# Attention and a two-layer MLP on one core: w_in loaded in parts between the first pairs, v of pair 0 on another queue, fewer zero matmuls, decay rows in front of q and k

## The chip, the core and the metric

The kernel runs on one core of a Trainium2 chip. Five engines run side by side, each through its own instructions in order: TensorE (PE), VectorE (DVE), ScalarE (ACT), GpSimd (POOL) and SyncE (SP). A transfer (DMA) is issued by SP, ACT or POOL into a queue of that engine, and all transfers run on 16 DMA engines. The metric is the device time of one execution in microseconds (us). The time of a kernel is the median of its runs.

## What is computed

Attention over 8 x 8 heads, 576 positions and 64 columns, with a decay from the running sum of a gate s, followed by two matrix products with a gated activation between them:

```python
cum = np.cumsum(np.maximum(s, 0.0), axis=-1)
bias = -(cum[:, :, :, None] - cum[:, :, None, :])
scores = np.where(causal, -1e9, q @ k.T / np.sqrt(D) + np.minimum(bias, 0.0))
attn = softmax(scores)
x = (attn @ v)                      # as 4608 tokens x 512
h = x @ w_in                        # 512 x 2048
out = (h * np.clip(h + 3, 0, 6) / 6) @ w_out
```

## The kernel before

**Units.** The 64 heads are worked as 32 pairs, two heads of one batch each. For a pair, q and k (f32, 288 KB each) come into one tile `qkf` (three buffers) and v (288 KB) into a slot of `v_f` (three slots, pair modulo 3). POOL casts q and k to f16 (`cast_qk`, L174), PE transposes them in two groups (`transpose_group`, L251), and DVE copies the result out of PSUM into `qkT`, again three slots. Rows 64 to 67 of a slot hold the decay: a running sum, split into three f16 parts, and its negative. They are worked out at the start for all heads. Pair 0 gets them straight from the tile `aug` (L475 to L482), pairs 1 to 9 from a scratch tensor in DRAM that `store_aug` (L486) fills in two halves and `load_aug` (L166) reads. Pairs from 10 on get theirs by another way.

`scores_bank` (L281) multiplies k and q of one head in four PSUM banks, ACT takes the exp of each bank into `Pm` (L299), and POOL clears what lies above the diagonal (L304). `attend` (L329) multiplies by v, whose cast `cast_v` is DVE's for pairs 0 to 3 and POOL's later, and divides. `x_transpose` (L365) puts the pair's result into `xT`. The first product, `m1` (L412), reads `xT` and `w_in`; the second, `m2`, reads `w_out`. Weights are cast from f32 to f16 on the way in, by DMAs that POOL issues: `w_in` in two halves of 1,024 columns (`load_w_in`, L391), each with four blocks of 128 rows, `w_out` in four parts.

**Order.** It is written out by hand (a manual schedule): each engine runs its instructions in the order in which the program names them. The start goes so:

1. SP loads s, and q and k of pairs 0 and 1; ACT loads the mask rows and the unit matrix. PE runs 18 zero matmuls (`keep_warm(18)`).
2. The decay is worked out on DVE. SP and ACT each issue four small DMAs for pair 0's rows (L475 to L482). Then SP asks for q and k of pair 2 and v of pair 0 (L483, L484).
3. POOL casts pair 0, PE transposes it, POOL stores the first half of the decay rows, SP loads them for pairs 1 and 2 and then v of pair 1, POOL casts pair 1, and PE runs `keep_warm(12)` (L659 to L670).
4. `first_tasks(p)` (L501) for pairs 0 to 3: scores of both heads, attention of the head before, the transposes of pair p + 1, and the loads ahead. Within pair 0, `casts` casts pair 2 behind pair 0's masks. Within pair 1 it casts v of pair 1, then q and k of pair 3, and then both halves of w_in are asked for (L524, L525).
5. `load_pair(6)`, casts of pair 4, three parts of w_out, four zero matmuls, the last head of pair 3 and its `x_transpose`.
6. The first eight column blocks of the first product over tokens 0 to 511 run in one piece (L685). After that attention and products are woven: `weave` (L617) takes attention tasks by their costs in proportion to the products' tasks.

`load_pair` (L492) is used for pairs 4 to 9 and names q and k first, then v, and the decay rows last, all on SP.

Of the kernel before, what the change touches and what calls it, by code (L numbers as in the profile page):

```python
# [16 lines left out]
def kernel(  # L17
# [10 lines left out]
    nc = tc.nc  # L28
# [9 lines left out]
    KC = DM // 128  # L38
# [6 lines left out]
    PTD = 10  # L45
# [7 lines left out]
    def bank():  # L53
        return psum.tile([128, 512], F32, tag="M", bufs=2, name="bank")
# [38 lines left out]
    w_in_sb = [  # L93
        cpool.tile([128, KC, 1024], F16, tag=f"c_win{h}", name=f"w_in{h}") for h in range(2)
    ]
# [11 lines left out]
        out=s8, in0=s_sb, scalar1=0.0, scalar2=8.0, op0=ALU.max, op1=ALU.mult  # L107
# [3 lines left out]
        out=c8, data0=s8, data1=s8, initial=0.0, op0=ALU.add, op1=ALU.max  # L111
# [12 lines left out]
        out=kaug[:, 2, :], in0=r1, in1=kaug[:, 1, :], op=ALU.subtract  # L124
# [18 lines left out]
    def load_qk(p, *engs):  # L143
        b, h0 = (2 * p) // H, (2 * p) % H
        t = work.tile([128, NTR, 2, D], F32, tag="qkf", bufs=3, name=f"qkf{p}")
        for i, src in enumerate((q, k)):
            rows = src[b, h0:h0 + 2].rearrange("h s d -> (h s) d")
            engs[i % len(engs)].dma_start(
                out=t[:, :, i, :], in_=rows.rearrange("(t p) d -> p t d", p=128)
            )  # L150
        qk_f[p] = t

    def load_v(p, eng):
        b, h0 = (2 * p) // H, (2 * p) % H
        sl = p % NS
        for hh in range(2):
            eng.dma_start(
                out=v_f[:, sl, hh, 0:4, :],
                in_=v[b, h0 + hh, 0:512].rearrange("(t p) d -> p t d", p=128),
            )  # L160
        eng.dma_start(
            out=v_f[0:64, sl, :, 4, :],
            in_=v[b, h0:h0 + 2, 512:SEQ].rearrange("h p d -> p h d"),
        )

    def load_aug(p, eng):  # L166
        sl = p % NS
        src, c0 = (aug_drams[0], p * W2) if 2 * p < NA else (aug_drams[1], p * W2 - NA * SEQ)
        eng.dma_start(
            out=qkT[64:68, sl, 0:2 * W2].rearrange("r (i c) -> r i c", i=2),  # L170
            in_=src[:, :, c0:c0 + W2].rearrange("i r c -> r i c"),
        )

    def cast_qk(p):  # L174
        t = work.tile([128, NTR, 2, D], F16, tag="qkh", bufs=2)
        nc.gpsimd.tensor_copy(out=t, in_=qk_f.pop(p))  # L176
        qk_h[p] = t
# [57 lines left out]
    def cast_v(p):  # L235
        sl = p % NS
        copy = nc.vector.tensor_copy if p < 4 else nc.gpsimd.tensor_copy
        copy(out=v_h[:, sl, :, :, 0:D], in_=v_f[:, sl])  # L238
# [12 lines left out]
    def transpose_group(p, g):  # L251
        t0, t1 = ((0, 5), (5, 9))[g]
        n = (t1 - t0) * 128
        pT = half_bank(p < 4)
        src = qk_h[p]
        for t in range(t0, t1):
            c = (t - t0) * 128
            transpose_tile(pT[:, c:c + 128], src[:, t, :, :], t == t0, t == t1 - 1)
        sl = p % NS
        c0 = t0 * 128  # L260
        for dst, r0 in ((qT, 0), (kT, 64)):
            nc.vector.tensor_copy(out=dst[0:64, sl, c0:c0 + n], in_=pT[r0:r0 + 64, 0:n])  # L262
        if g == 1:
            qk_h.pop(p)
# [64 lines left out]
    def attend(hd):  # L329

        p, hh = hd // 2, hd % 2
        sl = p % NS
        P = Pm[:, hd % NS, :]
        if hh == 0:
            O_tiles[p] = psum.tile([128, 2, 512], F32, tag="O", bufs=1, name=f"O{p}")
        O = O_tiles[p]
        for qt in range(5):
            for kt in range(qt + 1):
                c = BLOCK[kt, qt]
                nc.tensor.matmul(  # L340
                    out=O[:, hh, qt * VW:qt * VW + D + 1],
                    lhsT=P[:, c:c + 128],
                    rhs=v_h[:, sl, hh, kt, 0:D + 1],
                    start=(qt == 0),
                    stop=(qt == 4 and kt == 4),
                )
        if hh == 1:
            Ov = O_tiles.pop(p)[:, :, 0:5 * VW].rearrange("p h (t e) -> p h t e", t=5)
            r = work.tile([128, 2, 5, 1], F32, tag="r")
            nc.vector.reciprocal(out=r, in_=Ov[:, :, :, D:D + 1])  # L350
            xs = work.tile([128, 5, 2, D], F16, tag="xs", name=f"xs{p}")
            nc.vector.tensor_tensor(  # L352
                out=xs.rearrange("p t h d -> p h t d"),
                in0=Ov[:, :, :, 0:D],
                in1=r.to_broadcast([128, 2, 5, D]),
                op=ALU.mult,
            )
            x_tiles[p] = xs
# [6 lines left out]
    def x_transpose(p):  # L365
        b, hp = p // (H // 2), p % (H // 2)
        xs = x_tiles.pop(p)
        if by_dma(p):

            nc.sync.dma_start(  # L370
                out=xT[:, hp, b * SEQ:b * SEQ + 640].rearrange("p (t c) -> p t c", c=128),
                in_=xs.rearrange("p t h d -> p (t h d)"),
                transpose=True,
            )
            return
        pX = half_bank(p < 3)
        for qt in range(5):
            nc.tensor.matmul(
                out=pX[:, qt * 128:(qt + 1) * 128],
                lhsT=xs[:, qt, :, :],  # L380
                rhs=ident,
                is_transpose=True,
                start=(qt == 0),
                stop=(qt == 4),
            )
        nc.vector.tensor_copy(out=xT[:, hp, b * SEQ:(b + 1) * SEQ], in_=pX[:, 0:SEQ])
# [1 line left out]

    def load_w_in(h):  # L391
        nc.gpsimd.dma_start(
            out=w_in_sb[h],
            in_=moe_w_in[:, h * 1024:(h + 1) * 1024].rearrange("(kc p) f -> p kc f", p=128),
        )

    def load_w_out(c):
# [64 lines left out]
    def keep_warm(n):  # L462
        pw = bank()
        for i in range(n):
            nc.tensor.matmul(  # L465
                out=pw, lhsT=warm[:, 0:128], rhs=warm, start=(i == 0), stop=(i == n - 1)
            )
# [11 lines left out]
    for hh in range(2):  # L479
        c0, c1 = hh * SEQ, (hh + 1) * SEQ  # L480
        nc.sync.dma_start(out=kT[65:66, 0, c0:c1], in_=kaug[hh:hh + 1, 1, :])
        nc.scalar.dma_start(out=kT[66:67, 0, c0:c1], in_=kaug[hh:hh + 1, 2, :])  # L482
    load_qk(2, nc.sync)  # L483
    load_v(0, nc.sync)  # L484

    def store_aug(i, h0, h1, eng):  # L486
        eng.dma_start(
            out=aug_drams[i].rearrange("i r (h t) -> h (i r) t", t=SEQ),
            in_=aug[h0:h1].rearrange("h i r t -> h (i r) t"),
        )  # L490

    def load_pair(p):  # L492
        load_qk(p, nc.sync)
        load_v(p, nc.sync)
        if p < PTD:
            load_aug(p, nc.sync)

    def scores(hd):
        return [(lambda bi=bi: scores_bank(hd, bi), 400) for bi in range(4)]

    def first_tasks(p):  # L501

        def loads():
            if p == 0:
                load_qk(3, nc.sync)
                load_v(2, nc.sync)
            elif p > 1:
                load_pair(p + 2)  # L510

        def v_first():
            cast_v(0)
            load_v(3, nc.sync)
            load_aug(3, nc.sync)
            store_aug(1, NA, 2 * PTD, nc.sync)

        def casts():
            if p > 0:
                cast_v(p)  # L520
            if p < 2:
                cast_qk(p + 2)
            if p == 1:
                load_w_in(0)  # L524
                load_w_in(1)  # L525

        tr = [[], []]
        if p < 3:
            tr = [[(lambda: transpose_group(p + 1, 0), 640)],
                  [(lambda: transpose_group(p + 1, 1), 512)]]  # L530
        t = scores(2 * p)
        if p == 1:
            t += [(v_first, 0), (lambda: attend(0), 1200)]
        t += tr[0]
        if p > 0:
            t += [(lambda: attend(2 * p - 1), 1200)]
        t += scores(2 * p + 1) + [(casts, 0)] + tr[1]
        if p > 0:
            t += [(lambda: x_transpose(p - 1), 640)]
            t += [(lambda: attend(2 * p), 1200)]  # L540
        return [(loads, 0)] + t
# [125 lines left out]
        load_aug(p, nc.sync)  # L667
    load_v(1, nc.sync)
    cast_qk(1)
    keep_warm(12)  # L670
    for p in range(4):
        run(first_tasks(p))
    load_pair(6)
    cast_qk(4)
    cast_v(4)
# [59 lines left out]
```

The softmax here doesn't subtract the row's maximum and nothing guards it: scores larger than these inputs give would overflow.

## Time and profile before

| | |
|---|---|
| runs | 6, from 375.24 to 377.73 us, median 376.86 us |
| profiled execution | 375.24 us, of which the span of the profile is 373.5 us |
| clock granted to TensorE | 0.997 |
| PE busy | 353.8 us, 95% of the span |
| ACT, DVE, POOL busy | 209.4, 188.4 and 149.9 us |
| moved by DMA | 59.36 MB, 159 GB/s over the span |

PE is the busiest engine, and from about 100 us on it is busy almost without a break. Idle time of another engine costs nothing unless PE waits for it. By ten-microsecond stretches PE is busy 7.65 us from 40 to 50 us, 9.00 from 50 to 60, 9.53 from 60 to 70 and 8.71 from 70 to 80, and mostly 9.8 to 10.0 afterwards. In the first 34 us it has gaps of up to 1.45 us.

A few times of the start, from the timeline: the 18 zero matmuls run from 1.39 to 7.87 us, pair 0 is cast from 7.50 to 9.26, the twelve zero matmuls start at 10.85, the first score matmul at 13.45, the first exp at 13.82, and the first product with w_in at 34.08.

Times are in us from the start of the span. In the lines of the profile PEld is PE's weight load, and a name with a q behind it (SPq, ACTq, POOLq) is the issuing side of that engine. Matmuls are pipelined and their ends are modelled.

### The profile page before, as it was taken

How to read it: one execution, taken by the hardware profiler on the slowest of the kernel's cores; microseconds unless marked ns; L12 is line 12 of the kernel's file. 1: busy time of each engine (PE TensorE's matmuls, PEld its weight loads, DVE VectorE, ACT ScalarE, POOL GpSimd, SP SyncE). 2: the span in 40 equal slices, each digit the busy share in tenths (PEclk: the TensorE clock that was granted, in tenths of full speed). 3: DMA queues.
4: the chain of work that ended last, by engine and by line, in shares of the span. 5: the costliest groups of instructions: out<-in, count | busy, mean ns of one | idle time of the engine just before them, and what ended most of it. 6: DMA issues, size and time to landing. Idle time of an engine off the chain costs nothing.

```text
span 373.5 us, 7607 instructions
## 1 busy us (share of the span) xinstructions
PE 353.8 (95%) x2784; PEld 218.7 (59%) x2784; DVE 188.4 (50%) x331; ACT 209.4 (56%) x404; POOL 149.9 (40%) x378
## 2 busy tenths in 40 slices
PE   6778879999999899999999999999999999999995
PEld 2465555556666566566656665666566656555542
DVE  4685765666632455345533553455345545554531
ACT  4465764237884677477747774677467715443310
POOL 6582444354566355445544444444444300000000
PEclk9999999999999999999999999999999999999998
DMA  9699999946999999998999889889995101010012
GB/s 162 141 176 208 205 208 209 235 124 150 185 199 210 215 218 191 210 225 189 190 232 210 176 177 236 201 180 195 219 178 110 49 29 45 13 56 30 28 57 85
DMA packets 184526, 59.36 MB, mean 159 GB/s; under 512 B 177840, under 2 KB 178064, under 8 KB 184488
## 3 DMA queue, kind: packets, MB, share of 16 engines
q1 hardware_dynamic: 182392, 54.42, 69.6%
q0 software_dynamic: 1680, 4.27, 6.4%
q8 instruction: 22, 0.36, 0.4%
q10 hardware_dynamic: 416, 0.19, 0.2%
q14 instruction: 16, 0.13, 0.1%
HBM read 37.49 MB, written 9.62 MB: 126 GB/s over the span
## 4 chain that ended last, share of the span: by engine, by line
PE 83%; ACT 5%; DVE 4%; DMA 3%; issue 2%; POOL 1%; SPq 0%; ACTq 0%; POOLq 0%
PE bank L423 26%; PE po L445 23%; PE S L291 10%; PE bank L445 9%; PE O L340 7%; PE bankS L423 4%; ACT Pm L299 3%; DMA qkT<-xb 2%; ACT trl L431 1%; DMA qkf<-in_k_dram 1%; DVE gT L432 1%; DVE qkT L262 1%; PE bank L465 1%; PE bankY L423 1%; DVE xs L352 1%
## 5 line engine op out<-in xcount | busy, mean ns | idle before, releaser
L299 ACT ACTIVATE Pm<-S 128x384 f16<-128x384 f32 (+2 forms) x256 | 115.5, 508 | 57.3 <-PE S L291 52.9
L432 DVE SCALAR_TENSOR_TENSOR gT<-trl,bank 128x512 f16<-128x512 f32 x123 | 84.5, 687 | 102.2 <-ACT trl L431 101.9
L304 POOL TENSOR_SCALAR_AFFINE_SELECT Pm<-Pm 128x128 f16<-128x128 f16 (+2 forms) x256 | 79.3, 312 | 133.5 <-ACT Pm L299 123.7
L431 ACT ACTIVATE trl<-bank,bias 128x512 f32<-128x512 f32 x123 | 85.2, 693 | 77.3 <-PE bank L423 75.5
L423 PE MATMUL bank<-xT,w_in 128*128 128x512 f16 x492 | 126.4, 382 | 0.7
L445 PE MATMUL po<-w_out_sb,gT 128*128 128x512 f16 x416 | 104.3, 379 | 0.0
L423 PEld LDWEIGHTS <-w_in 128*128 128x128 f16 x576 | 78.5, 146 | 33.4 <-issue 2.4
L445 PEld LDWEIGHTS <-gT 128*128 128x128 f16 x576 | 52.3, 98 | 48.6 <-issue 0.3
L291 PE MATMUL S<-qkT 128*128 128x320 f16 (+4 forms) x448 | 70.2, 261 | 7.1 <-ACT Pm L299 4.1
L291 PEld LDWEIGHTS <-qkT 128*128 128x128 f16 x448 | 40.9, 98 | 36.6 <-issue 4.3
L340 PEld LDWEIGHTS <-Pm 128*128 128x128 f16 x960 | 38.3, 97 | 13.2 <-POOL Pm L304 1.8
L340 PE MATMUL O<-v_h,Pm 128*128 128x65 f16 x960 | 40.8, 193 | 1.5 <-POOL Pm L304 1.3
L445 PE MATMUL bank<-w_out_sb,gT 128*128 128x512 f16 x160 | 39.4, 379 | 0.0
L352 DVE TENSOR_TENSOR xs<-O,r 128x640 f16<-128x640 f32 x32 | 26.4, 825 | 1.1
L454 DVE TENSOR_SCALAR osb<-po 128x512 f32<-128x512 f32 x26 | 17.9, 688 | 15.2 <-PE po L445 14.9
L222 POOL CAST xb<-qkf 128x1152 f16<-128x1152 f32 x22 | 25.3, 1149 | 0.0
L238 POOL CAST v_h<-v_f 128x640 f16<-128x640 f32 x28 | 20.1, 719 | 3.1 <-DMA v_f<-in_v_dram 3.1
L454 DVE TENSOR_SCALAR osb<-bank 128x512 f32<-128x512 f32 x10 | 6.9, 691 | 26.0 <-PE bank L445 26.0
L176 POOL CAST t<-qkf 128x1152 f16<-128x1152 f32 x10 | 12.4, 1241 | 12.2 <-DMA qkf<-in_k_dram 12.2
L423 PE MATMUL bankS<-xT,w_in 128*128 128x512 f16 x64 | 16.4, 379 | 0.0
L431 ACT ACTIVATE trl<-bankS,bias 128x512 f32<-128x512 f32 x16 | 11.0, 688 | 8.0 <-PE bankS L423 8.0
L432 DVE SCALAR_TENSOR_TENSOR gT<-trl,bankS 128x512 f16<-128x512 f32 x16 | 11.0, 688 | 6.8 <-ACT trl L431 6.8
(49 smaller groups left out, 120.2 us busy)
## 6 DMA issues: line engine op xcount, KB each, us to landing
qkf<-in_q_dram SPq DMA_DIRECT2D x32, 288.0 KB, 4.3
qkf<-in_k_dram SPq DMA_DIRECT2D x32, 288.0 KB, 4.2
out_dram<-osb SPq DMA_DIRECT2D x36, 256.0 KB, 2.8
v_f<-in_v_dram SPq DMA_DIRECT2D x64, 128.0 KB, 4.1
w_in<-in_moe_w_in_dram POOLq DMA_DIRECT2D x2, 1024.0 KB, 12.0
w_out_sb<-in_moe_w_out_dram POOLq DMA_DIRECT2D x4, 512.0 KB, 7.9
v_f<-in_v_dram SPq DMA_DIRECT2D x32, 32.0 KB, 2.7
qkT<-xb SPq DMA_TRANSPOSE x22, 4.9
```

The source lines that it names most:

```text
L222: nc.gpsimd.tensor_copy(out=x.rearrange("p (i t) c -> p t i c", i=2)[:, :, :, 0:D], in_=qk_f.pop(p))
L238: copy(out=v_h[:, sl, :, :, 0:D], in_=v_f[:, sl])
L291: nc.tensor.matmul(out=S[:, c:c + hi - lo], lhsT=kT[:, sl, off + 128 * kt:off + 128 * (kt + 1)], rhs=qT[:, sl, off + lo:off + hi], start=( ...
L299: nc.scalar.activation(out=P[:, p0:p0 + n], in_=S[:, 0:n], func=AF.Exp, scale=0.125, bias=0.0)
L304: nc.gpsimd.affine_select(out=view, in_=view, pattern=pattern, compare_op=ALU.is_ge, fill=0.0, base=0, channel_multiplier=-1,)
L340: nc.tensor.matmul(out=O[:, hh, qt * VW:qt * VW + D + 1], lhsT=P[:, c:c + 128], rhs=v_h[:, sl, hh, kt, 0:D + 1], start=(qt == 0), stop=(qt ...
L352: nc.vector.tensor_tensor(out=xs.rearrange("p t h d -> p h t d"), in0=Ov[:, :, :, 0:D], in1=r.to_broadcast([128, 2, 5, D]), op=ALU.mult,)
L423: nc.tensor.matmul(out=ph, lhsT=w_in_t[f // 8][:, kc, f % 8, :], rhs=xT[:, kc, n * 512:(n + 1) * 512], start=(kc == 0), stop=(kc == KC - 1),)
L431: nc.scalar.activation(out=trl, in_=ph, func=AF.Relu, bias=bias3[:, 0:1], scale=1.0)
L432: nc.vector.scalar_tensor_tensor(out=gT[n][:, f, :], in0=trl, scalar=6.0, in1=ph, op0=ALU.min, op1=ALU.mult)
L445: nc.tensor.matmul(out=po, lhsT=gT[n][:, f, t4 * 128:(t4 + 1) * 128], rhs=w_out_sb[:, f, :], start=(f == 0), stop=(f == NF - 1),)
L454: nc.vector.tensor_scalar_mul(out=osb, in0=po, scalar1=1.0 / 6.0)
```

## The change

Four edits, all in the start of the kernel and in `load_pair`:

- `load_w_in` takes a range of row blocks. The first block of the first half is asked for by POOL after the cast of pair 1, the second in `casts` of pair 0, in front of the cast of pair 2. The other two blocks and the second half are asked for where both halves stood.
- v of pair 0 goes on ACT's queue, and its three issues stand ahead of the load of pair 2.
- `keep_warm(12)` becomes `keep_warm(6)`.
- `load_pair` names the decay rows first, then q and k, then v.

```diff
-    def load_w_in(h):
+    def load_w_in(h, k0=0, k1=KC):
         nc.gpsimd.dma_start(
-            out=w_in_sb[h],
-            in_=moe_w_in[:, h * 1024:(h + 1) * 1024].rearrange("(kc p) f -> p kc f", p=128),
+            out=w_in_sb[h][:, k0:k1, :],
+            in_=moe_w_in[:, h * 1024:(h + 1) * 1024].rearrange("(kc p) f -> p kc f", p=128)[
+                :, k0:k1, :
+            ],
         )
...
+    load_v(0, nc.scalar)
     load_qk(2, nc.sync)
-    load_v(0, nc.sync)
...
     def load_pair(p):
+        if p < PTD:
+            load_aug(p, nc.sync)
         load_qk(p, nc.sync)
         load_v(p, nc.sync)
-        if p < PTD:
-            load_aug(p, nc.sync)
...
             if p > 0:
                 cast_v(p)
+            if p == 0:
+                load_w_in(0, 1, 2)
             if p < 2:
                 cast_qk(p + 2)
             if p == 1:
-                load_w_in(0)
+                load_w_in(0, 2, 4)
                 load_w_in(1)
...
     cast_qk(1)
-    keep_warm(12)
+    load_w_in(0, 0, 1)
+    keep_warm(6)
     for p in range(4):
         run(first_tasks(p))
```

## The prediction

> **What bounds the kernel now.** I read the page first: TensorE (PE) is 95% busy over a span of 373.5 us, so a change in the loads can only pay where PE waits. Of PE's waits most lie before 34 us (2.0 us on exps, 1.6 on casts, 1.2 + 0.8 on xs, 0.9 before the zero matmuls) and between 42 and 80 us, and from 90 us on the list holds 1.5 us in all. All that the change touches lies before 45 us, so the chain of waits there comes next, start, length and what:
>
> ```profile
> 10.30 0.50 DVE qkT L262
> 10.81 0.05 issue
> 10.85 2.76 PE bank L465 x12
> 13.62 0.18 PE S L291 x2
> 13.79 0.02 issue
> 13.82 3.29 ACT Pm L299 x8
> 17.11 0.32 PE S L291 x2
> 17.43 1.47 POOL t L176
> 18.89 0.05 issue
> 18.94 0.45 PE pTm L247 x5
> ```
>
> No load stands in it. After pair 0's transposes come twelve zero matmuls, eight exps of pair 0 back to back, then GpSimd's (POOL's) cast of pair 2, on which PE's next transposes wait. From there the chain alternates between PE, exps and VectorE (DVE) until 34.24, where the first product with w_in starts straight after the last transpose of x. The timeline of POOL shows why its cast is in the chain: POOL has no gap from 14.38 to 19.94 us.
>
> ```profile
> 14.38 3.08 POOL L304 TENSOR_SCALAR_AFFINE_SELECT Pm<-Pm 128x256 f16<-128x256 f16 x8 [3.26 <-ACT Pm L299]
> 17.41 1.47 POOL L176 CAST t<-qkf 128x1152 f16<-128x1152 f32 x1
> 22.32 1.14 POOL L176 CAST t<-qkf 128x1152 f16<-128x1152 f32 x1
> 23.41 1.54 POOL L392 DMA_DIRECT2D w_in<-in_moe_w_in_dram x2
> 40.59 1.14 POOL L176 CAST t<-qkf 128x1152 f16<-128x1152 f32 x1 [9.24 <-DMA qkf<-in_k_dram]
> ```
>
> The last line is the second place: the cast of pair 4 waits 9.24 us for its load and ends at 41.73, and the weight loads of pair 4's transposes wait for it:
>
> ```profile
> 41.79 0.62 PEld L247 LDWEIGHTS <-t 128*128 128x128 f16 x9 [0.16 <-POOL t L176]
> ```
>
> Only 0.16 us here, but with nothing to spare. The DMA view of 23 to 36 us says why pair 4 is late (queue, packets, MB, share of the engines; then issues with their time to landing): w_in's queue q0 holds the engines, and SyncE's (SP's) q1 gets a fifth.
>
> ```profile
> q0 software_dynamic: 899, 1.81, 79.9%
> q1 hardware_dynamic: 1549, 0.48, 20.0%
> ...
> w_in<-in_moe_w_in_dram POOLq DMA_DIRECT2D x2, 1024.0 KB, 12.0
> qkf<-in_q_dram SPq DMA_DIRECT2D x1, 288.0 KB, 15.0
> ```
>
> SP is held inside its issues meanwhile (timeline of SP):
>
> ```profile
> 24.95 2.72 SPq L148 DMA_DIRECT2D qkf<-in_k_dram  x1
> 27.76 11.26 SPq L157 DMA_DIRECT2D v_f<-in_v_dram  x2
> ```
>
> The two w_in halves land 9.0 and 15.0 us after their issues, at 32.4 and 39.2; their users start at 34.08 and 42.4, so w_in itself is not waited for.
>
> **What the Trainium skill says.** "DMA: Bandwidth & Descriptors", section "Queues, rings and completion order": each DMA engine goes round its queues packet by packet. The trace agrees: 899 large packets of q0 took 79.9% while 1,549 small ones of q1 took 20.0%. "Trainium Kernel Development and Optimization", "Key Constraints": issuing from another engine "only saves the sequencer's issue time", as the transfers share the same 16 engines. So v on ScalarE's (ACT's) queue frees SP, but brings no bandwidth. "TensorE: Matmul & The Clock Gate", Part 1: the clock falls after an idle window of about 3.4 us; in the trace weight loads of zero matmuls stand 0.43 us apart until 6 us, and PE then runs at full rate through idle stretches of up to 1.45 us.
>
> **The change part by part**, against the profiled execution (375.24 us: span 373.5 and 1.74 around it).
>
> *Half as many zero matmuls.* Twelve take 2.76 us with the drain, 0.216 us each in the chain's spacing (2.6/12), so six fewer let PE go 1.3 us sooner, at 12.15. But pair 0's scores also need the decay rows: the last row issued on ACT's queue starts at 9.54 and takes 3.3 us, so 12.85; SP's last starts at 9.79, and with 2.7 to 3.3 us lands at 12.5 to 13.1. The first score matmul stood at 13.45, its weights at 13.24. So the gain is 0.15 to 0.6 us; I take 0.35. What is late next is the rows. PE's new idle gap is under 1 us, far from the clock's window.
>
> *v of pair 0 on ACT's queue.* Three issues of 0.6 us (ACT's own in the rows: 0.54 to 0.66) from 10.20 end at about 12.1; queued behind them are pair 0's exps, which start at 13.4 or later: free. SP is rid of 1.67 + 0.70 us, so pair 1's rows can be asked for once their store has landed (9.21 + 3.5 = 12.7 instead of 14.63), then v of pair 1, pair 3 and so on, each up to 2.4 us sooner. None of these is in the chain.
>
> *First quarter of w_in, after the cast of pair 1.* POOL is free from 11.13 to 14.38, so its issue costs nothing there. Its price lies in the DMA engines: 256 KB (as written) at the 206 GB/s of the w_in stretch are 1.25 us, I take 1.5. The engines bring pair 2 and v of pair 0 (576 + 288 KB at 240 GB/s, 3.6 us) from 12.1 on: done at 15.7 before, at 17.2 with the quarter (flow from about 13.3, as w_in's flow began some 2.2 us after its issue). Pair 2's cast will ask at 17.66 (next part), so 0.4 us are left. Pair 1's rows come behind pair 2 in q1, at 17.4, where scores of head 2 would like to start at 16.75 and started at 17.09 before. This costs 0 to 0.3 us there, but PE's transposes wait for the cast anyhow.
>
> *Second quarter, in front of the cast of pair 2.* This issue is on the chain. The trace has no issue of this size: w_in halves hold POOL for 0.755 to 0.787 us, w_out's four for 0.551 to 0.561. A quarter of a half has the fewest rows: I take 0.55, bounds 0.3 and 0.8. Below nothing is excluded. Behind it wait the cast, the transposes of pair 2 and head 1's attention. Cast at 17.46 - 0.35 + 0.55 = 17.66: 0.2 us later than before. Its traffic (flow 19.4 to 21.5) moves pair 3 to about 22.3, where the cast asks at 22.5. Of w_in's remaining two issues one is smaller, saving 0.1 us, hidden.
>
> *Three quarters of w_in left.* From 26 us, 13.2 us of flow become 9.9, so w_in ends at 35.7 and not 39.2, pair 4 lands near 36.5 and its cast is 4 us ahead of PE. In the profiled execution this returns only the 0.16 us.
>
> *Decay rows in front.* Rows of pair 4 write the slot that head 3's scores read (done at 25.56) and read scratch that SP stores just before (3.5 us to land): SP waits there till about 26, and q, k and v of pair 4 are queued behind, 1.5 us later than at 24.50. Hidden under w_in's flow, which holds them till 36 anyway. Later rows (pairs 7 to 9) wait for scores of three pairs back, done by then at 48.8, 58.5 and 66.7: nothing, since q and k of pair 7 were asked for at 56.77 only, and SP runs 4 us sooner at most.
>
> Sum: -0.35 + 0.55 + 0 - 0.16 = 0.0 us: 375.3 for an execution like the profiled one. But that was the fastest of six, 1.6 us under the median of 376.86. As pair 4 has no slack, slower DMA there goes straight into the time; I estimate that half of the 1.6 us is this and comes back. So 376.86 + 0.0 - 0.8 = **376.1 us**.
>
> **The rivals.**
> *More comes back.* All 1.6 us of the spread are pair 4's, the zero matmuls give 0.6, POOL's issue 0.3 on the chain: 376.86 - 1.6 - 0.6 + 0.3 - 0.16 = 374.8. For it: nothing else on the edge in the profiled execution ends in a load before 90 us. Against it: a wait for a transposed pair at 124 us (1.0 us) varies too.
> *Quarters crowd out pairs 2 and 3, slower.* Place: POOL's casts at 17.66 and 22.5. If a quarter costs 3 us of engine time beside two small-packet queues (twice my figure), pair 2 lands at 18.7 and pair 3 slips by about as much: +1.0 each, +0.2 for the late score rows, -0.5 of relief: 376.86 + 1.7 = 378.6. It decides from the point where pair 2 lands after 17.7. For it: q1 got only a fifth beside w_in. Against it: a quarter is short, and engines were idle at 16 to 17 us (busy share 0.32).
> *The gap in front of pair 0's scores does nothing*: rows are bound and POOL's issue costs 0.8: +0.65, inside the forecast's spread.
>
> **How the numbers follow.** Forecast 0.48, more back 0.28, crowding 0.24. What can be told from no change is about 0.3%, 1.1 us. Of the forecast's 0.48, 0.12 lies below 375.7; of crowding 0.04 ends within. Faster 0.40, same 0.40, slower 0.20. The forecast's own range is 375.2 to 377.0; eight in ten need 374.2 to 378.4.
>
> **What would show it.** First exp at 13.3 to 13.7; pair 2's cast at 17.5 to 17.9 with an issue of about 0.55 us before it and no wait for a load; first w_in product at 33.9 to 34.5; POOL's wait for pair 4 ending by 37; PE's waits after 45 us as they were. A cast of pair 2 or 3 that waits for its DMA says crowding; a first w_in product before 33.5, or PE's waits beyond 45 us shrinking, would make the forecast wrong on the other side.

## The result, and the profile after

| | before | after |
|---|---|---|
| median | 376.46 us (37 runs, 374.95 to 381.74) | 380.0 us (16 runs, 379.0 to 382.13) |
| ratio | | 1.0091 [1.0071, 1.0111] |
| profiled execution, its span | 375.24, 373.5 us | 379.0, 377.3 us |
| first product with w_in starts | 34.08 us | 37.94 us |
| from there to the end of the span | 339.4 us | 339.4 us |

The change made the kernel 0.9% slower, above the predicted range (374.2 to 378.4). The last two lines say where: all 3.8 us are lost before the first product, and nothing comes back later. PE's waits behind the first product are the same rows with the same sums in both (2.0 us on exps, 1.6 on qkT's copies, 1.3 on masks). Some executions of any version are over 1.5% longer than its fastest, and the ratios leave these out, as the starts compared below leave out the profiled execution of e8, which is one of them.

The chain of waits of the kernel after, at the place where twelve zero matmuls and exps stood before (start, length, what):

```profile
10.69 0.97 ACTq L157
...
12.47 7.03 DMA v_f<-in_v_dram
19.50 0.04 DVEq L238
19.54 0.04 issue
19.58 0.51 DVE v_h L238
20.09 1.48 PE S L291 x7
```

A load now stands in the chain, for 7 us: the last part of v of pair 0, 32 KB from ACT's queue. It is one of three: pair 2 is cast from 19.89, as soon as it has landed, and the scores of head 2 start at 20.07. These don't read v; they need q and k of pair 1, copied by 17.2, and pair 1's decay rows. So the rows are the likelier thing that they wait for, though the trace, which gives no landing for them here, names the cast of v that ends at the same moment. POOL's timeline shows the casts of pairs 2, 3 and 4 (before: 17.41, 22.32 and 40.59):

```profile
12.05 0.54 POOL L392 DMA_DIRECT2D w_in<-in_moe_w_in_dram  x1
...
16.96 0.55 POOL L392 DMA_DIRECT2D w_in<-in_moe_w_in_dram  x1
19.89 1.18 POOL L176 CAST t<-qkf 128x1152 f16<-128x1152 f32 x1 [2.38 <-DMA qkf<-in_k_dram]
...
26.21 1.15 POOL L176 CAST t<-qkf 128x1152 f16<-128x1152 f32 x1
27.30 1.50 POOL L392 DMA_DIRECT2D w_in<-in_moe_w_in_dram  x2
...
43.97 1.15 POOL L176 CAST t<-qkf 128x1152 f16<-128x1152 f32 x1 [8.51 <-DMA qkf<-in_k_dram]
```

The cast of pair 2 waits 2.38 us for its load. Pair 3 is cast 3.89 us later than before, and as many later the rest of w_in is asked for, so pair 4 waits for its load as it did (8.51 us, 9.24 before). The queues' view of 10 to 20 us (packets, MB, share of the 16 engines), of the kernel before:

```profile
q1 hardware_dynamic: 6017, 1.52, 69.8%
q0 software_dynamic: 48, 0.07, 7.3%
q10 hardware_dynamic: 64, 0.00, 0.4%
```

and of the kernel after:

```profile
q0 software_dynamic: 285, 0.52, 36.3%
q1 hardware_dynamic: 2956, 0.76, 35.6%
q10 hardware_dynamic: 1264, 0.30, 13.5%
```

The sums are the same, 1.60 and 1.58 MB. But 0.45 MB more of it is w_in, which the kernel before first uses at 34.08 us, and so SP's and ACT's queues (q1, q10), with what PE waits for, brought 1.06 MB, not 1.52. SP's timeline of the kernel before:

```profile
14.63 0.82 SPq L169 DMA_DIRECT2D qkT<-aug_scratch  x2
15.50 0.95 SPq L157 DMA_DIRECT2D v_f<-in_v_dram  x2
16.50 0.65 SPq L161 DMA_DIRECT2D v_f<-in_v_dram  x1
17.25 0.54 SPq L148 DMA_DIRECT2D qkf<-in_q_dram  x1
```

and after:

```profile
13.83 1.01 SPq L169 DMA_DIRECT2D qkT<-aug_scratch  x2
14.89 4.09 SPq L157 DMA_DIRECT2D v_f<-in_v_dram  x2
19.02 0.70 SPq L161 DMA_DIRECT2D v_f<-in_v_dram  x1
19.82 0.54 SPq L148 DMA_DIRECT2D qkf<-in_q_dram  x1
```

SP does ask for pair 1's rows 0.8 us sooner. Then two issues of v of pair 1 hold it for 4.09 us (0.95 before), and pair 3 is asked for 2.57 us later. The list of SP's waits names a load of `v_f`, and the ones under way then are those of pair 0, on ACT's queue:

```profile
SPq L157 <- DMA v_f<-in_v_dram: 3.3, 1, 3.3
```

### The profile page after: what moved, and what is told of

It reads as the page before. It is cut to its first block, busy times and chain, and to the rows that moved or that the text cites. A ratio compares the mean times of both kernels' runs of the same rounds, so it can differ in the third digit from the quotient of the medians.

```text
span 377.3 us, 7596 instructions
## 1 busy us (share of the span) xinstructions
PE 354.1 (94%) x2778; PEld 219.9 (58%) x2778; DVE 190.1 (50%) x331; ACT 209.7 (56%) x404; POOL 149.5 (40%) x380
## 4 chain that ended last, share of the span: by engine, by line
PE 83%; DVE 5%; DMA 4%; ACT 4%; issue 2%; ACTq 1%; POOL 1%; POOLq 0%; DVEq 0%
PE bank L425 26%; PE po L447 23%; PE S L291 11%; PE bank L447 9%; PE O L340 7%; PE bankS L425 4%; ACT Pm L299 2%; DMA v_f<-in_v_dram 2%; DMA qkT<-xb 2%; ACT trl L433 1%; DVE gT L434 1%; DVE qkT L262 1%; PE bankY L425 1%; DMA s_sb<-in_s_dram 1%; PE pT L378 1%
## 5 line engine op out<-in xcount | busy, mean ns | idle before, releaser
L291 PE MATMUL S<-qkT 128*128 128x320 f16 (+4 forms) x448 | 71.3, 265 | 11.2 <-DVE v_h L238 3.8
L340 PEld LDWEIGHTS <-Pm 128*128 128x128 f16 x960 | 39.2, 99 | 12.9 <-POOL Pm L304 1.8
L340 PE MATMUL O<-v_h,Pm 128*128 128x65 f16 x960 | 41.6, 195 | 1.5 <-POOL Pm L304 1.3
L456 DVE TENSOR_SCALAR osb<-po 128x512 f32<-128x512 f32 x26 | 17.9, 688 | 15.2 <-PE po L447 14.9
L176 POOL CAST t<-qkf 128x1152 f16<-128x1152 f32 x10 | 11.5, 1150 | 14.2 <-DMA qkf<-in_k_dram 14.2
## 6 DMA issues: line engine op xcount, KB each, us to landing
w_in<-in_moe_w_in_dram POOLq DMA_DIRECT2D x1, 1024.0 KB, 14.1
```

The source lines that it names most:

```text
L291: nc.tensor.matmul(out=S[:, c:c + hi - lo], lhsT=kT[:, sl, off + 128 * kt:off + 128 * (kt + 1)], rhs=qT[:, sl, off + lo:off + hi], start=( ...
L340: nc.tensor.matmul(out=O[:, hh, qt * VW:qt * VW + D + 1], lhsT=P[:, c:c + 128], rhs=v_h[:, sl, hh, kt, 0:D + 1], start=(qt == 0), stop=(qt ...
L456: nc.vector.tensor_scalar_mul(out=osb, in0=po, scalar1=1.0 / 6.0)
```

## Experiments

All ratios are against runs of the kernel before on the same chip, taken together with them: their medians were 375.6 us for e1 to e8, 375.55 for e9 to e11 and 376.53 for e12, so a median of the table isn't to be set against 376.46. A ratio isn't the quotient of two medians either. That is up to 0.3% off (1.0033 for e1, 1.0077 for e7) and lies within the interval each time, so differences of 0.2% between two ratios aren't read.

| kernel | median us | ratio | pair 3 cast at | first product at |
|---|---|---|---|---|
| before | 376.46 | 1 | 22.32 | 34.08 |
| after | 380.0 | 1.0091 [1.0071, 1.0111] | 26.21 | 37.94 |
| e1 after, quarters undone | 376.87 | 1.0012 [0.9986, 1.0037] | 23.42 | 35.23 |
| e2 after, v back on SP | 379.32 | 1.0082 [1.0051, 1.0114] | 25.32 | 37.06 |
| e3 before + quarters | 378.14 | 1.0065 [1.0043, 1.0087] | 25.42 | 37.16 |
| e4 before + v on ACT | 376.86 | 1.0027 [1.0004, 1.0051] | 24.03 | 36.55 |
| e5 before + first quarter | 377.61 | 1.0041 [1.0022, 1.0060] | 25.95 | 37.47 |
| e6 before + second quarter | 377.52 | 1.0040 [1.0019, 1.0060] | 25.66 | 37.92 |
| e7 after, twelve zeros again | 378.52 | 1.0049 [1.0017, 1.0081] | 26.89 | 38.61 |
| e8 before + six zeros | 376.92 | 1.0035 [1.0009, 1.0062] | – | – |
| e9 e3 + pair 1's rows on ACT | 378.76 | 1.0063 [1.0035, 1.0091] | 25.22 | 37.99 |
| e10 before + rows first | 375.53 | 1.0009 [0.9983, 1.0034] | 23.17 | 34.91 |
| e11 before + six zeros + fewer row DMAs | 376.78 | 1.0019 [0.9990, 1.0049] | 23.88 | 36.98 |
| e12 e7 + fourteen zeros in the stall | 379.6 | 1.0074 [1.0047, 1.0101] | 26.19 | 37.91 |

The last two columns are from one profiled execution each. A single execution is not its kernel's median: e10's first product is 0.8 us later than that of before, and its median is the same within its interval.

### Which of the four edits

e1 takes both early quarters out of the changed kernel:

```diff
-    load_w_in(0, 0, 1)
     keep_warm(6)
...
-            if p == 0:
-                load_w_in(0, 1, 2)
...
-                load_w_in(0, 2, 4)
+                load_w_in(0)
```

> The changed kernel with w_in asked for in two halves at the old place; v of pair 0 on ACT's queue, six zero matmuls and the early decay rows stay. Theory 1 (the quarters take the DMA engines from pair 2, v of pair 0 and pair 1's rows): all land some 2.5 us sooner, the first product starts at 34 to 34.8 instead of 37.94, median 376 to 377. Theory 2 (v on ACT's queue is the cause: shared bandwidth and SP's issues held by it): nothing comes back, 379.3 to 380.3, first product near 37.9. Theory 3 (half as many zero matmuls let PE's clock fall): about 379 with the clock still at 0.5 somewhere before 26 us.

e2 puts v of pair 0 back behind pair 2 on SP's queue:

```diff
-    load_v(0, nc.scalar)
     load_qk(2, nc.sync)
+    load_v(0, nc.sync)
```

> The changed kernel with v of pair 0 back on SP behind q and k of pair 2; the quarters, six zero matmuls and early decay rows stay. Theory 1 (quarters): stays slow, 378.5 to 380, PE still waits about 3 us for scores of head 2. Theory 2 (v on ACT's queue): back to 376 to 377, SP's wait before the second decay rows gone and pair 2 asked for near 10.3 instead of 11.18. Theory 3: about 379.

e3 is the kernel before with the quarters alone (the edit of e1 the other way round, with `keep_warm(12)`):

> The kernel before with the early quarters of w_in alone. Theory 1: 378.5 to 380, pair 2 lands after 18.5 and PE stalls before scores of head 2. Theory 2 and theory 3: 376 to 377.3, at most the 0.55 us that the second quarter's issue holds POOL.

e4 is the kernel before with v of pair 0 alone on ACT's queue (the edit of e2 the other way round):

> The kernel before with v of pair 0 on ACT's queue alone. Theory 1: 375.8 to 377. Theory 2: 378.5 to 380, with SP's issues of pair 2 later than 10.32 and v of pair 1 held. Both parts needed (a fourth reading): e3 and e4 each lose less than 1.2 us and their sum is well under the 3.5 us.

Without the quarters 0.12% is left of 0.91%, within the interval of nothing; the quarters alone cost 0.65%, at 378.14 us a little less than theory 1 expected. The edit of v costs 0.27% alone, and undoing it in the changed kernel gains nothing that can be told (1.0082 against 1.0091): once the quarters hold the loads up, the other queue changes little. e1 loses 1.2 us in its profiled start, where no quarter is involved: its scores of head 2 start at 18.27 us (before: 17.09). The zero matmuls (below) are one suspect, and v is another, for e4, with twelve of them, starts head 2 at 18.25.

e7 gives the changed kernel its twelve zero matmuls back; e8 is the kernel before with the opposite edit alone, six in place of twelve:

```diff
-    keep_warm(6)
+    keep_warm(12)
```

> The changed kernel with twelve zero matmuls. If the number of zero matmuls is what lets PE's clock fall: clock at 1.00 until 20 us and a gain of 0.8 us or more over the changed kernel (379 or less). If it is PE's stall before scores of head 2 that does: clock still at 0.5 for about 6 us after the stall, 379.5 to 380.5.

> The kernel before with six zero matmuls alone. As predicted: scores of pair 0 start 0.15 to 0.6 us sooner, or wait for their rows, and the time is within 0.6 us of before. If the gap cools the clock: 0.5 us or more slower, with a clock under 1.00 in 14 to 18 us.

e10 is the kernel before with the decay rows in front in `load_pair`, and nothing else:

```diff
     def load_pair(p):
+        if p < PTD:
+            load_aug(p, nc.sync)
         load_qk(p, nc.sync)
         load_v(p, nc.sync)
-        if p < PTD:
-            load_aug(p, nc.sync)
```

> The kernel before with the decay rows named first in the loads of pairs 4 to 9 alone. As predicted: hidden, within 0.5 us of before. If SP's wait for the stored rows matters: slower by up to 1.5 us with pair 4 landing later than 40.5. If the other three parts' losses of e1 are made up by this part: faster by 0.5 to 1 us.

Fewer zero matmuls cost 0.35% alone; they gain nothing. Undoing them gives 1.0049 against 1.0091, with intervals that overlap, and e7's profiled start is even later than that of the changed kernel, so their share there isn't settled. e10 shows the decay rows to be free, to 0.3%. The parts alone sum to 0.65 + 0.27 + 0.35 + 0.09 = 1.36%, together 0.91%. Each part is known to about 0.2%, so these sums don't show that the parts share a delay; they allow it.

PE's timeline of e1 shows what the six zeros bought:

```profile
10.05 1.47 PE L465 MATMUL bank<-warm 128*128 128x512 f16 x6 [0.86 <-DVE qkT L262]
13.85 0.73 PE L291 MATMUL S<-qkT 128*128 128x256 f16 x6 [2.33 <-DMA qkT<-aug]
```

PE waits 2.33 us for pair 0's decay rows, and its scores start at 13.85, later than the 13.45 of the kernel before. And the granted clock drops behind that gap. Stretches of 1 us of e1, with busy time of PE, PEld, DVE, ACT and POOL, then the clock, the DMA share (which can pass 1) and GB/s:

```profile
13.00:14.00 1.00, 0.15 (x2) 0.17 (x3) 0.15 (x1) 0.00 (x0) 0.00 (x0) 1.00 1.02 232
14.00:15.00 1.00, 0.83 (x8) 0.53 (x7) 0.00 (x0) 0.79 (x2) 0.23 (x1) 0.70 1.27 286
15.00:16.00 1.00, 1.00 (x10) 0.93 (x9) 0.25 (x1) 0.90 (x3) 0.74 (x4) 0.50 1.27 287
```

It stays at 0.5 until about 17.8 us, though no quarter is there to stop PE. In the kernel before the clock never falls in this part. The zero matmuls covered a wait. With six of them PE's scores stop for rows until 13.3 to 14.0 us in all four profiles (the changed kernel, e1, e2, e11); with twelve they stop until 13.7 to 14.1 in five (e4, e5, e7, e9, e12), and in e3, e6 and e10 run through from 12.7 or 12.8.

### The two quarters apart

e5 loads only the first quarter early (12 us), e6 only one at the later place, in front of the cast of pair 2 (17 us). The other three stay where both halves stood:

```diff
     cast_qk(1)
+    load_w_in(0, 0, 1)
...
-                load_w_in(0)
+                load_w_in(0, 1, 4)
```

> The kernel before with only the first early quarter of w_in (after the cast of pair 1); the other three blocks stay at the old place. Theory 1a (the quarter that flows from about 13.5 us holds up pair 1's decay rows, 18 KB behind pair 2 and v of pair 0 in SP's queue, and scores of head 2 wait for them): nearly all of the quarters' loss, 377.5 to 378.5, with PE waiting 2 to 3.5 us for those rows. Theory 1b (POOL's issue in front of the cast of pair 2, as the prediction had it): 375.5 to 376.5, no loss.

```diff
+            if p == 0:
+                load_w_in(0, 0, 1)
...
-                load_w_in(0)
+                load_w_in(0, 1, 4)
```

> The kernel before with only the second early quarter (one block of w_in, in front of the cast of pair 2). Theory 1a: within 0.8 us of before, since its flow begins after 18.5 us, when the rows have landed; the 0.55 us that it holds POOL at most. Theory 1b: 0.5 to 0.8 us slower. A loss over 1.2 us with a late pair 3 would say that pair 3's load is crowded instead.

Each costs 0.4%, by another way, so the first isn't nearly all of the loss, as theory 1a had it. With the first, the queues of 12 to 17 us in e5 read

```profile
q1 hardware_dynamic: 2629, 0.66, 59.3%
q0 software_dynamic: 153, 0.27, 36.5%
```

where before had 0.98 MB in q1. The quarter took 1.8 us of the engines (36.5% of 5), and q1 fell 0.32 MB behind. This agrees with the arbitration that the Trainium skill states in "DMA: Bandwidth & Descriptors", section "Queues, rings and completion order", each engine going round its queues packet by packet: the quarter is asked for at 11.65, behind q and k of pair 2 (10.36 and 11.20), and doesn't wait for them; pair 2, there by 17.41 in the kernel before, is cast at 18.78 after 2.0 us of waiting. SP was late too; it was held in its third issue of v of pair 0 (e5's timeline of SP):

```profile
14.21 3.39 SPq L161 DMA_DIRECT2D v_f<-in_v_dram  x1
17.71 0.82 SPq L169 DMA_DIRECT2D qkT<-aug_scratch  x2
...
20.32 0.54 SPq L148 DMA_DIRECT2D qkf<-in_q_dram  x1
```

so pair 1's rows were asked for 3.1 us later than before, and pair 3 as well. The scores of head 2 waited 4.2 us for the rows. Why the issue took 3.39 us isn't shown: the list of SP's waits names nothing for it, and the kernel before spent 0.70 on the same issue with the engines busier (DMA share 1.20 from 13 to 14 us there, 0.99 in e5 from 14 to 15).

Nor is the hold needed. In e3, with both quarters, SP isn't held there (0.70 us) and asks for the rows at 14.74, as the kernel before does at 14.63. Its chain:

```profile
14.74 4.41 DMA qkT<-aug_scratch
19.15 0.14 issue
19.28 1.49 PE S L291 x7
...
25.18 0.29 POOL Pm L304
25.47 1.11 POOL t L176
```

The rows take 4.41 us, and the scores of head 2 start 2.2 us later than in the kernel before. In e6, which has no quarter at that time, rows asked for at 14.77 were there by 16.96. Pair 2 is on time in e3 (cast at 17.30, no wait), and pair 3 is cast late not for its load but for the masks of the late scores, with PE's clock at 0.50 from 18 to 24 us.

With the second quarter alone (e6), pair 2 and head 2 are on time (17.23 and 16.96), and pair 3 is asked for as before, at 17.38. But (e6's chain)

```profile
17.96 7.58 DMA qkf<-in_k_dram
...
25.66 1.15 POOL t L176
```

k of pair 3 takes 7.58 us to land; in the kernel before, asked for at 17.83, it was there by 22.32, so it took 4.5 at most. In e10, also without a quarter, it was asked for at 17.91, and POOL waited for it until 23.17:

```profile
23.17 1.14 POOL L176 CAST t<-qkf 128x1152 f16<-128x1152 f32 x1 [1.28 <-DMA qkf<-in_k_dram]
```

So it took some 5.2 us there, and by this estimate one 256 KB quarter beside it costs 2.3 us by e10 and 3.1 or more by the profile of the kernel before. This quarter is asked for at 16.64, just ahead of q and k (17.38 and 17.96), so here its place in time alone could have put it first.

### Are pair 1's rows the gate?

In e3 the scores of head 2 wait 3.5 us for the rows, and in the changed kernel 3.8, most likely for the same. e9 is e3 with these rows on ACT's queue, ahead of the loads:

```diff
-    for p in (1, 2):
-        load_aug(p, nc.sync)
+    load_aug(1, nc.scalar)
+    load_aug(2, nc.sync)
```

> The kernel before with both early quarters, as in e3, but pair 1's decay rows (18 KB) are asked for on ACT's queue and not behind pair 2 and v of pair 0 on SP's. Theory R (PE's stall before scores of head 2 is these rows, stuck in SP's queue while the quarter flows): the wait of 3.5 us falls under 1 us, scores of head 2 start by 17.5, and the next thing that is late is v of pair 0 or the cast of pair 2 at 18 to 19; 1 to 2 us come back of the 2.5, 376 to 377.2. Theory G (the quarters make everything late alike, the rows are only the first of it): what PE gains on the rows it loses on v of pair 0, 377.6 to 378.5.

The rows are asked for at 13.53 and not 14.74, head 2 starts at 18.55 and not 19.28, and the time is that of e3 (1.0063); the median, 378.76, lies 0.3 us above the range of theory G. e9's chain says why:

```profile
13.53 4.89 DMA qkT<-aug_scratch
...
18.90 6.20 DMA qkf<-in_k_dram
25.22 1.15 POOL t L176
...
26.83 4.31 DMA qkT<-aug_scratch
```

18 KB take 4.89 us even when asked for early and on another queue than q, k and v, and pair 3 is the next gate, then pair 3's own rows. So it isn't one transfer that was in the wrong place; all of them are late.

e11 tries to save the six zeros' gain: in the kernel before, pair 0's three rows of k come in one DMA for each head, with six zero matmuls:

```diff
-        nc.sync.dma_start(out=kT[64:65, 0, c0:c1], in_=kaug[hh:hh + 1, 0, :])
...
-        nc.sync.dma_start(out=kT[65:66, 0, c0:c1], in_=kaug[hh:hh + 1, 1, :])
-        nc.scalar.dma_start(out=kT[66:67, 0, c0:c1], in_=kaug[hh:hh + 1, 2, :])
+        nc.sync.dma_start(out=kT[64:67, 0, c0:c1], in_=kaug[hh:hh + 1, :, :][:, 0:3, :])
...
-    keep_warm(12)
+    keep_warm(6)
```

> The kernel before with six zero matmuls, and pair 0's three k rows of a head in one DMA on SP (two DMAs instead of two on ACT and four on SP, after the last row is worked out). If pair 0's scores are bound by its rows and by SP's issues waiting for free semaphores, the rows land near 11.6, scores start near 12 with no gap that cools the clock, and pair 2 is asked for near 9.5: 0.8 to 1.5 us faster than before, 374.2 to 375. If what follows (pair 1's rows, POOL) takes it back: 375 to 376.

The rows land at 13.34, because they are worked out late (SP can issue from 9.14 on), and PE still waits 1.3 us for them. No gain: 1.0019, which includes nothing. In its profiled execution w_in itself was waited for at last (1.18 us at 36.98), as in e4 (0.55): these kernels ask for w_in at 25.0 and 25.1, and so w_in itself can come last. Whether the quarters lift that limit no run here tells: in every kernel with both of them the first product is later than 37 us for other reasons.

### Loads or clock?

The granted clock of the changed kernel is 0.50 from 16 to 25 us, in the 3.8 us stall and behind it, and first products come 17.9 us after the scores of head 2, not 17.0 as before. e12 tests whether the clock is the price of those 0.9 us. It is e7 with fourteen zero matmuls inside the stall:

```diff
             t += [(lambda: attend(2 * p), 1200)]
+        if p == 0:
+            t += [(lambda: keep_warm(14), 0)]
```

> The changed kernel with twelve zero matmuls in front of pair 0's scores (as in e7) and fourteen more between the last transposes of pair 1 and the scores of head 2, where PE stood still for 3.5 us in e7. They take about 3.0 us at full clock (0.216 us each) and lie inside that wait, so no load and no cast is moved. Theory C (the loads set when head 2's scores start, some 3 us late, and the lowered clock after the stall costs about 0.9 us more): scores of head 2 start at 20.1 to 20.7 as before, the granted clock stays at 0.95 or more from 16 to 26 us (0.50 at 22 to 24 in e7), the first product with w_in comes 17.0 us after those scores, not 18.0 as in e7 (at 37.1 to 37.6, not 38.61), and the time falls 0.6 to 1.0 us below e7's: ratio 1.002 to 1.004 against e7's 1.0049. Rival L (the late loads, casts of pairs 2 and 3 and v alone set every start up to 38 us, the clock is only a symptom): the clock stays up, but the first product stays at 38.3 or later and the ratio at 1.005 or more. If the fillers themselves push the scores back (a bank of PSUM not free, or more than the stall holds), the scores start after 21 us and the run tells neither.

The clock was held, and the scores of head 2 start at 20.21, as they should. Stretches of 2 us of e7 (the number before the last two is the clock; those are the DMA share and GB/s):

```profile
20.00:22.00 2.00, 1.17 (x12) 0.90 (x13) 0.44 (x1) 1.00 (x3) 1.50 (x2) 0.86 1.01 164
22.00:24.00 2.00, 2.00 (x36) 2.00 (x34) 0.62 (x2) 0.69 (x2) 0.82 (x3) 0.50 1.23 276
```

and of e12:

```profile
20.00:22.00 2.00, 1.60 (x27) 1.38 (x28) 0.00 (x0) 1.42 (x4) 1.71 (x3) 1.00 0.92 191
22.00:24.00 2.00, 1.70 (x29) 1.30 (x26) 1.72 (x4) 1.38 (x4) 1.00 (x4) 1.00 1.27 261
```

The time did not fall: 1.0074, where e7 has 1.0049 (the intervals overlap), and the first product is at 37.91, where the changed kernel has 37.94. That start is sooner than e7's 38.61, but meets neither window, 37.1 to 37.6 or 38.3 and later; it comes 17.7 us after the scores of head 2, not 17.0. By the time, theory C is wrong for this kernel, and the rival holds. What is late next shows in e12's timeline of POOL:

```profile
26.19 1.14 POOL L176 CAST t<-qkf 128x1152 f16<-128x1152 f32 x1 [1.14 <-DMA qkf<-in_k_dram]
```

With PE at full clock POOL is ready 1.14 us before pair 3 is there and waits for it, which was asked for at 19.72 and 20.30. In the changed kernel the masks of slow PE's exps end at the same 26.2. Two limits lie at one place, and lifting the clock alone showed no gain.

The table shows how the start is tied together: the first product starts 11.5 to 11.8 us after the cast of pair 3 begins, in nine of its thirteen starts. In the other four (e4, e6, e9, e11) it is 12.3 to 13.1 us; in three of them PE waits again on the way, for w_in (0.55 us in e4, 1.18 in e11) or for pair 3's rows (0.88 in e9). The cast of pair 3 is where the delays meet, and not their cause: in the kernel before, the changed one, e1, e3 and e4 it doesn't wait for its load but comes behind POOL's masks, which follow the scores and exps; in the others it waits for the load, from 0.23 us (e7) to 3.97 (e6).

## Why the prediction was wrong

**The step that failed: "First quarter of w_in, after the cast of pair 1", and with it the traffic of the second.** 1.25 us of engine time for 256 KB, taken as 1.5, were to put pair 2 at 17.2 and pair 1's rows "behind pair 2 in q1, at 17.4", where "This costs 0 to 0.3 us", and the second quarter was to move pair 3 "to about 22.3". Measured: the first quarter uses 1.8 us of the engines, not far from the 1.5, and pair 2 is even cast at 17.30 without a wait in e3 (18.78 in e5, 19.89 with all edits). But scores of head 2 start at 18.6 to 20.6 us in every kernel with the first quarter, at 19.28 in e3 after a wait of 3.5 us for the rows. And pair 3, with the second quarter alone, is cast at 25.66 (e6). So a load behind a quarter comes 2 to 3 us late for about 2 us of engine time. The sum divided bytes by the engines' rate, as if the quarter were one more item in a line. It had no term for a small load that takes longer beside it (the rows: 4.41 us in e3, 2.2 at most in e6), and none for SP, which can be held in an issue (3.39 us in e5), so that later requests also start late. What part of the delay is taken by w_in's packets and what by the last engine to end isn't settled.

**The rival "Quarters crowd out pairs 2 and 3, slower" was right**, and it had the size of the delay: 3 us per quarter, pair 2 at 18.7 (e5: 18.78). But it reckoned these as 3 us of engine time, which measured 1.8 in e5 and 2.2 in e6 (27.7% of 16 to 24 us), and in e3 not pair 2 but the rows behind it are late; that the delay came out near its figure is in part luck. Its sum was +1.7 us; the quarters alone gave 0.65%, some 2.4 us, and all edits 0.91%, some 3.4 us. It allowed for 1.0 us at each cast, where pair 3 alone moved 3.1 to 3.9, counted on 0.5 of relief, had 0.2 for the late rows, which came 2 to 3 us late, and had nothing for the other edits. It was given 0.24.

**"v of pair 0 on ACT's queue": "SP is rid of 1.67 + 0.70 us" and so sooner by up to 2.4 us, with "None of these is in the chain": false on both counts.** Alone (e4) the edit gave SP nothing: it asked for k of pair 2 2.1 us later, at 13.53, for the rows of pair 1 only 0.6 us sooner, and for pair 3 at 17.24 as before (17.25). With the quarters SP asked for pair 3 2.57 us later, because its issue of v of pair 1 waits for a load on ACT's queue, and pair 3 is in the chain as soon as it is late. Pair 3 is at the edge already in the kernel before: e10, with the same start, waited 1.28 us for it at 23.17. For ACT it wasn't "free" either: in the changed kernel the three issues end at 13.16, not 12.1, and the first exp stands behind them, at 13.20. Alone this edit costs 0.27%. That a second queue "only saves the sequencer's issue time" was cited from the Trainium skill ("Trainium Kernel Development and Optimization", "Key Constraints"); here it didn't save that either.

**"Half as many zero matmuls": -0.35 us: wrong in sign.** PE was let go at 11.80, sooner than worked out (12.15), but the last rows landed at 14.0 in the changed kernel, 13.8 in e1, 13.34 in e11, not at 12.85 to 13.1. DVE's last step for them takes 0.75 us in the profiled execution of before, which the prediction read, and 1.58 to 1.72 in every other profile; in the changed kernel their issues came later, at 9.50 and 9.99 us. Whether that is all of it isn't settled. "PE's new idle gap is under 1 us, far from the clock's window" was off twice: 1.52 us, and enough. Alone it costs 0.35%. The remark "rows are bound" among the rivals had the mechanism, and reckoned with a lost gain, not with a loss.

**Right:** the second quarter's issue, 0.55 us in front of the cast of pair 2 (0.55), and 0.54 for the first; the decay rows in front, nothing (e10: 1.0009), though SP waits for them until 27.5 us there, not 26, and asks for pair 4 3.4 us later, not 1.5; PE's waits behind the start as they were.

**"Three quarters of w_in left", and 0.8 us that come back with pair 4: didn't come.** The rest is asked for behind the cast of pair 3, at 27.30 and not 23.41, so pair 4 is as late as ever. Nor is that edge worth what was put on it. In the thirteen profiles of the table pair 4 is cast between 2.9 us (e9) and 7.2 us (e10) after the first product begins, and the span from there on is 338.4 to 339.8 us in all, without a trend.

**Not settled:** how the loss divides where several limits lie together; whether e7's ratio, lower than e12's and than that of the changed kernel, is more than the spread (their intervals overlap). No version tried is shown to be faster than the kernel before; the decay rows in front are the one edit of the four that alone costs nothing that can be told.

## What to carry to other kernels

A load that is asked for early isn't free because the engines seem idle on average: count what else must land in the same few microseconds, and price it by how far it pushes the *last* of these, including the requests that the issuing engine can only make later. Before moving an issue to another queue, look which waits the issues of both engines share. And look for the event in which the delays meet (here a cast, 11.7 us ahead of the first product in most profiles): an edit pays only if that event moves.

## What the runs showed of the hardware that wasn't expected

- The clock falls after short gaps. The Trainium skill's "TensorE: Matmul & The Clock Gate", Part 1, puts the fall after an idle window of about 3.4 us. In the changed kernel the clock has begun to fall before 16 us (0.81 from 15 to 16), and the longest stop between 9 us and then is 1.52 us; in e1 it was at 0.70 from 14 to 15, after one of 2.33 us; in e9, with twelve zero matmuls, at 0.77 from 18 to 20, after one of 1.82 us. The kernels with no stop over 1.45 us there (before, e10 and e12) kept it, and e2 and e11 kept it through stops of 1.33 and 1.31. So here the measurement decides against the page's figure. But the length of a stop isn't the whole of it: stops of 1.71 us in e1 and 1.75 in e7 that ended at about 8.6 us were followed by a clock of 1.00 until 14 and 21. A stall of 4 us that was filled with zero matmuls left it at 1.00 (e12).
- Loads of the same size differ by the company they have: 288 KB of k landed in at most 4.5 us (before) and some 5.2 (e10) beside SP's own queue, and in 7.58 us beside one 256 KB load of w_in (e6); 18 KB of rows were there after 2.2 us (e6) or took 4.41 (e3) and 4.89 (e9).
- SP's and ACT's issues aren't independent: with v of pair 0 on ACT's queue, an issue of SP waited 3.3 us for it to land in the changed kernel, and SP's second pair of decay rows waited for k of pair 1 and went out at 9.68 to 10.04 us in all five profiles with v there (the changed kernel, e1, e4, e7, e12). With v on SP it went out at 8.53 to 8.79 in before, e2, e3, e5, e6, e9 and e10. What the two share isn't shown.
